# Attention scores as keys by queries in 32-row tiles, with K in natural order and projections of a whole head group

## Chip, cores and metric

The kernel runs on one core of one Trainium2 chip. The metric is the device time of one execution in microseconds (us). A run that is over 1.5% above the fastest of its kernel is called slow, and only fast runs are compared.

Names of the engines: PE is TensorE's matmul side, PEld its weight load, DVE is VectorE, ACT is ScalarE, POOL is GpSimd, SP is SyncE.

## The reference

```python
B, Sq, D = 8, 112, 640
H, Sk, Dh = 32, 512, 192                      # bf16 everywhere
q = (x @ wq).reshape(B, Sq, H, Dh).transpose(0, 2, 1, 3)
scores = einsum("bhqd,bhkd->bhqk", q, k_cache) * Dh ** -0.5
p = softmax(scores)
o = einsum("bhqk,bhkd->bhqd", p, v_cache)
out = o.transpose(0, 2, 1, 3).reshape(B, Sq, H * Dh) @ wo
```

K and V are 50 MB each and every byte of them is used once. The projections are small beside them in bytes, but not in TensorE time: in the kernel before they take 1.55 of the 3.64 us that a pair of heads takes (by the starts of the matmuls, O 3 x (216 + 55) ns and Q 15 x 49).

## The kernel before

The kernel before works on pairs of heads. It computes scores as queries by keys. K comes through a transposing DMA, so that the head dimension lies on the partitions. The four score matmuls of a head contract over 2 x 128 rows although a head has only 192: part of each is padding. The exponentials are then turned round by matmuls against a diagonal matrix that also divides by the sum, and evicted by ScalarE (one head) and VectorE (the other), before PV can use them.

```python
def pe_S(pe, i):                      # scores of two heads, queries x keys
    ...
        pe.matmul(bk[:, 0:256], qs[:, qb, EA[h], :], ktb[:, :, 0, cs], start=True, stop=False)
        pe.matmul(bk[:, 0:256], qs[:, qb, ET[h], :], ktb[:, :, 1, cs], start=False, stop=True)
        pe.matmul(bk[:, 256:512], qs[:, qb, OC[h], :], ktb[:, :, 2, cs], start=True, stop=False)
        pe.matmul(bk[:, 256:512], qs[:, qb, OH[h], :], ktb[:, :, 1, cs], start=False, stop=True).then_inc(sS, 1)

def pe_PT(pe, ip, h):                 # turn the exponentials round
    ...
    for j in range(4):
        mm = pe.matmul(ps[:, 2 + h, j * SQ:(j + 1) * SQ], p_sb[:, pslot, j * 128:(j + 1) * 128],
                       dg[:, dslot, :], start=True, stop=True)

def pe_Q(pe, ip):                     # query projection of two heads, transposed
    ...
    for c in range(3):
        for dc in range(DC):
            lhsT = wq_sb[:, wb, dc, c0 + 128 * c:c0 + 128 * (c + 1)]
            mm = pe.matmul(ps[:, 5, c * SQ:(c + 1) * SQ], lhsT, xT_sb[:, dc, b * SQ:(b + 1) * SQ],
                           start=(dc == 0), stop=(dc == DC - 1))
```

Of the kernel before, what the change touches and what calls it, by code (L numbers as in the profile page):

```python
# [5 lines left out]

BF16 = mybir.dt.bfloat16
F32 = mybir.dt.float32
ACTF = mybir.ActivationFunctionType
ALU = mybir.AluOpType  # L10

DEFAULT_ORDERS = dict(
    PE=[("S", 0), ("PT0", -1), ("PV", -2), ("PT1", -1), ("O", -3), ("Q", 2)],
# [7 lines left out]
def build_mha_kernel(nc, x, k_cache, v_cache, wq, wo, out, cfg=None):  # L21
    cfg = dict(cfg or {})
    B, SQ, D = x.shape
    _, H, SK, DH = k_cache.shape
# [3 lines left out]
    DC = D // 128  # L28
# [8 lines left out]
    scale = float(DH) ** -0.5  # L37
# [31 lines left out]

    with ExitStack() as es:  # L70
        def sb(name, shape, dt):
            return es.enter_context(nc.sbuf_tensor(name, shape, dt))

        def sem(name):
            return es.enter_context(nc.semaphore(name))

        WQC = HG * DH
        wq_sb = sb("wq_sb", [128, 2, DC, WQC], BF16)
        wo_sb = sb("wo_sb", [128, 2, 3 * PPU, D], BF16)
        OUTT = cfg.get("OUTT", False)  # L80
        if OUTT:
            accT = sb("accT", [128, B, DC, SQ], F32)
            oTf = sb("oTf", [128, 2, DC, SQ], BF16)
            acc = None
        else:
            acc = sb("acc", [SQ, B, D], F32)
        xT_sb = sb("xT_sb", [128, DC, B * SQ], BF16)
        kt = [sb(f"kt{j}", [128, 2, 3, G * 128], BF16) for j in range(NKB)]
        vt = [sb(f"vt{j}", [128, G, 768], BF16) for j in range(NVB)]
        qs = sb("qs", [128, NQ, NSLOT, SQ], BF16)  # L90
        s_sb = sb("s_sb", [SQ, NSS, SK], F32)
        p_sb = sb("p_sb", [SQ, NP, SK], BF16)
# [4 lines left out]
        ident = sb("ident", [128, 128], BF16)  # L97
        nmx = sb("nmx", [SQ, NS], F32)
        rsum = sb("rsum", [SQ, NS], F32)
        rinv = sb("rinv", [SQ, NS], F32)  # L100
        ps = es.enter_context(nc.psum_tensor("ps", [128, 8, 512], F32))

        sS = sem("sS"); sPT = sem("sPT"); sPV = sem("sPV"); sO = sem("sO"); sQ = sem("sQ")
        dSM = sem("dSM"); dDG = sem("dDG"); dQC = sem("dQC"); dPTE = sem("dPTE"); dOA = sem("dOA"); dRC = sem("dRC")
        aEX = sem("aEX"); aQE = sem("aQE"); aPTE = sem("aPTE"); aPVE = sem("aPVE")
        gI0 = sem("gI0"); gINIT = sem("gINIT"); dINIT = sem("dINIT")
        sOF = sem("sOF"); aOF = sem("aOF")
        mX = sem("mX")
# [4 lines left out]
        mK = [sem(f"mK{j}") for j in range(NKB)]  # L113
        mV = [sem(f"mV{j}") for j in range(NVB)]
        mOUT = [sem(f"mOUT{j}") for j in range(2)]
# [3 lines left out]
        mWQ = [sem(f"mWQ{j}") for j in range(min(2, NHG) * PPU)]  # L119
        mWO = [sem(f"mWO{j}") for j in range(min(2, NHG) * PPU)]  # L120
# [23 lines left out]
        block = es.enter_context(nc.Block())  # L144

        def W(eng, s, v):
            if v > 0:
                eng.wait_ge(s, v)
# [120 lines left out]
        def act_evacQ(act, ip):  # L269
            W(act, sQ, ip + 1)  # L270
            W(act, sS, 2 * (ip - NQ) + 2)
            act.activation(qs[:, ip % NQ, 0:3, :], ps[:, 5, 0:3 * SQ].rearrange("p (c s) -> p c s", c=3),  # L272
                           ACTF.Copy).then_inc(aQE, 1)

        def act_evacpT0(act, ip):
            W(act, sPT, 2 * ip + 1)
            W(act, sPV, ip - NPT + 1)
            act.activation(pT_sb[:, ip % NPT, 0, :], ps[:, 2, 0:4 * SQ], ACTF.Copy).then_inc(aPTE, 1)  # L278

        def act_exp(act, i, h):  # L280
            Hh = 2 * i + h
            W(act, dSM, Hh + 1)
            W(act, sPT, Hh - NP + 1)
            act.activation(p_sb[:, Hh % NP, :], s_sb[:, Hh % NSS, :], ACTF.Exp,  # L284
                           bias=nmx[:, Hh % NS:Hh % NS + 1], scale=-1.0,
                           accum_out=rsum[:, Hh % NS:Hh % NS + 1]).then_inc(aEX, 1)

        def act_evacPV(act, ip):
            W(act, sPV, ip + 1)
            W(act, sO, ip - NO + 1)  # L290
            act.activation(oT_sb[:, ip % NO, :, :], ps[:, 4, 0:3 * SQ].rearrange("p (c s) -> p c s", c=3),  # L291
                           ACTF.Copy).then_inc(aPVE, 1)

        def act_evacOF(act, ip):
# [3 lines left out]
            W(act, sOF, b + 1)  # L298
            act.activation(o_out[:, b, :], psb[0:SQ, 7, 256:256 + D], ACTF.Copy).then_inc(aOF, 1)

# [3 lines left out]
        def dve_diag(dve, ip, h):  # L304
# [3 lines left out]
            dve.tensor_scalar(dg[:, Hh % ND, :], ident[0:SQ, 0:SQ], rinv[:, Hh % NS:Hh % NS + 1], None,  # L308
                              op0=ALU.mult).then_inc(dDG, 1)

# [17 lines left out]
        def dve_smax(dve, i, h):  # L328
            Hh = 2 * i + h
            W(dve, sS, Hh + 1)  # L330
            W(dve, aEX, Hh - NSS + 1)
            dve.tensor_scalar(s_sb[:, Hh % NSS, :], ps[0:SQ, h, :], -scale, None, op0=ALU.mult,  # L332
                              op1=ALU.min, accum_out=nmx[:, Hh % NS:Hh % NS + 1]).then_inc(dSM, 1)

# [11 lines left out]
        def dve_oacc(dve, ip):  # L346
# [6 lines left out]
            if OUTT:  # L353
# [3 lines left out]
                for k, (src, cs) in enumerate(parts):  # L357
# [6 lines left out]
                    else:  # L364
                        ins = dve.tensor_tensor(dst, src, accT[:, b, cs, :], op=ALU.add)
                ins.then_inc(dOA, 1)
                return
            parts = [(ps[0:SQ, 6, :], slice(0, 512)), (ps[0:SQ, 7, 0:128], slice(512, 640))]
            for k, (src, cs) in enumerate(parts):
# [4 lines left out]
                elif hg < NHG - 1:  # L374
                    ins = dve.tensor_tensor(acc[:, b, cs], src, acc[:, b, cs], op=ALU.add)
                else:
                    ins = dve.tensor_tensor(o_out[:, b, cs], src, acc[:, b, cs], op=ALU.add)  # L377
            ins.then_inc(dOA, 1)
# [5 lines left out]
        psb = ps[:].bitcast(BF16)  # L384
# [27 lines left out]
        def run_program(eng, stages, order, hook=None, post_hook=None):  # L412
            for i in PER:
                if hook is not None:
                    hook(eng, i)
                for st, lag in order:
                    ip = i + lag
                    if ok(ip):
                        stages[st](eng, ip)
                if post_hook is not None:  # L420
                    post_hook(eng, i)
# [24 lines left out]
        def _(act):  # L446
            W(act, dINIT, 1)
            act.activation(dummy[:, 2:3], dummy[:, 0:1], ACTF.Exp)
            run_program(act, ACT_STAGES, orders["ACT"])
# [211 lines left out]
    return nc  # L661


def bass_standalone__mha_block_cached__near_ridge_kernel(
    nc: bass.Bass,
    x: bass.AP,
    k_cache: bass.AP,
    v_cache: bass.AP,
    wq: bass.AP,
    wo: bass.AP,  # L670
    out: bass.AP,
):
    return build_mha_kernel(nc, x, k_cache, v_cache, wq, wo, out)


# [26 lines left out]
```

## Time and profile before

| what | value |
|---|---|
| time, median of 3 runs | 500.46 us (500.19 to 501.19) |
| span of the profiled execution | 499.2 us |
| PE busy, VectorE busy, ScalarE busy | 96%, 89%, 71% |
| PE instructions, matmuls, weight loads and waits (single records) | 14,364 |
| packets of instructions (queue q8) | 56 |

The page of the kernel before, cut to lines that matter here. "busy" is the time and the share of the span, with the number of instructions. The two rows of digits cut the span into 40 slices: the granted TensorE clock, and the mean busy share of the DMA engines, in tenths. The queue row is packets, megabytes and share of 16 engines. The last line is the chain of work that ended last, by engine.

```profile
span 499.2 us, 18678 instructions
PE 479.0 (96%) x6824; PEld 418.9 (84%) x6824; DVE 446.6 (89%) x1610; ACT 355.1 (71%) x898; POOL 71.5 (14%) x133
PEclk9999999999999999999999999999999999999999
DMA  9999999999999999999999999999999999999000
q8 instruction: 56, 0.92, 0.8%
PE 93%; DMA 2%; issue 1%; DVE 1%; POOL 1%; ACT 0%; DVEq 0%; POOLq 0%; ACTq 0%
```

TensorE is busy nearly all the time at full clock (the clock record gives 1.0 for 471 us and 0.5 for the last 2.9), and it is 93% of the chain. So this kernel is bound by TensorE's work. The row "q8 instruction" is easy to pass over: 0.92 MB in 56 packets is 16 KB each, and 14,364 / 56 is 256 instructions of PE for each.

The timeline of PE in the kernel before, one line for each run of like instructions: start, duration, line, operation, output and inputs, shapes, count.

```profile
301.23 0.36 PE L182 MATMUL ps<-dg,p_sb 112*128 112x112 bf16 x4
301.43 0.56 PE L200 MATMUL ps<-pT_sb,vt 128*128 128x112 bf16 x8
301.92 0.39 PE L206 MATMUL ps<-pT_sb,vt 128*64 128x112 bf16 x8
```

The starts tell the price, as the records of matmuls overlap (L200's last 213 ns in the mean and start 49 ns apart at the median): L200 starts 0.49 us before L206 with eight matmuls of 112 columns, 61 ns each with the switch of tile shapes included. There is no pause between groups.

The longest waits of PE in the kernel before: instruction, what ended the wait, total us, times, longest.

```profile
PE ps L402 <- DMA vt<-in_x_dram: 7.2, 1, 7.2
PE ps L262 <- DMA wq_sb<-in_wq_dram: 5.2, 3, 1.9
PE ps L166 <- issue: 1.9, 5, 0.8
```

PE waits about 16 us in all, most of it for first loads. "issue" is time in which the engine waited for nothing that the profile shows; it is 1.9 us here.

### The profile page before, as it was taken

The numbers are of one execution on the slowest core, as the hardware profiler recorded it, in microseconds if no ns is written. First come the engines' busy times: TensorE is split into PE (matmuls) and PEld (weight loads), VectorE is DVE, ScalarE is ACT, GpSimd is POOL, SyncE is SP. The second block draws the span as 40 slices with busy tenths as digits, with TensorE's granted clock in tenths as the row PEclk, the third lists the DMA queues.
The fourth block names the chain that finished last, engine by engine and source line by source line (L and its number), as shares of the span: only waits on it lengthen the run. The fifth ranks groups of instructions, "written<-read, shape, count | busy, mean of one in ns | idle before, by whom it ended". The sixth has DMA issues, their size and how long they took to land.

```text
span 499.2 us, 18678 instructions
## 1 busy us (share of the span) xinstructions
PE 479.0 (96%) x6824; PEld 418.9 (84%) x6824; DVE 446.6 (89%) x1610; ACT 355.1 (71%) x898; POOL 71.5 (14%) x133
## 2 busy tenths in 40 slices
PE   1799999999999999999999999999999999999995
PEld 1788888888888888888888888888888888888884
DVE  2589999998999999999999999999999999999994
ACT  1277777777777777777777777777777777777773
POOL 7110133131000133131000122322000000000000
PEclk9999999999999999999999999999999999999999
DMA  9999999999999999999999999999999999999000
GB/s 227 305 285 239 244 256 274 249 265 292 237 249 263 281 261 259 245 265 251 239 247 236 259 290 279 240 282 260 233 272 254 255 260 255 238 258 261 3 14 25
DMA packets 239738, 119.90 MB, mean 240 GB/s; under 512 B 201840, under 2 KB 236480, under 8 KB 239648
## 3 DMA queue, kind: packets, MB, share of 16 engines
q1 hardware_dynamic: 233472, 101.82, 94.4%
q0 software_dynamic: 6176, 16.88, 11.3%
q8 instruction: 56, 0.92, 0.8%
q14 instruction: 34, 0.28, 0.2%
HBM read 67.21 MB, written 1.15 MB: 137 GB/s over the span
## 4 chain that ended last, share of the span: by engine, by line
PE 93%; DMA 2%; issue 1%; DVE 1%; POOL 1%; ACT 0%; DVEq 0%; POOLq 0%; ACTq 0%
PE ps L262 19%; PE ps L234 16%; PE ps L182 13%; PE ps L200 10%; PE ps L206 8%; PE ps L166 6%; PE ps L169 6%; PE ps L167 6%; PE ps L168 6%; PE ps L235 4%; DMA wq_sb<-in_wq_dram 2%; DVE xT_sb L409 1%; POOL wq_sb L578 0%; DVE s_sb L332 0%; DVE o_out L377 0%
## 5 line engine op out<-in xcount | busy, mean ns | idle before, releaser
L284 ACT ACTIVATE p_sb<-s_sb,nmx 112x512 bf16<-112x512 f32 x256 | 181.6, 712 | 3.1 <-DVE s_sb L332 2.1
L332 DVE TENSOR_SCALAR_CACHE_REDUCE s_sb<-ps 112x512 f32<-112x512 f32 x256 | 166.3, 686 | 16.2 <-PE ps L169 14.0
L278 ACT ACTIVATE pT_sb<-ps 128x448 bf16<-128x448 f32 x128 | 69.5, 543 | 88.4 <-PE ps L182 88.4
L262 PE MATMUL ps<-xT_sb,wq_sb 128*128 128x112 bf16 x1920 | 118.0, 215 | 5.2 <-DMA wq_sb<-in_wq_dram 5.2
L234 PE MATMUL ps<-wo_sb,oT_sb 128*112 128x512 bf16 x384 | 118.3, 380 | 0.0
L262 PEld LDWEIGHTS ps<-xT_sb,wq_sb 128*128 128x128 bf16 x1920 | 103.8, 99 | 16.7 <-DMA wq_sb<-in_wq_dram 4.4
L182 PE MATMUL ps<-dg,p_sb 112*128 112x112 bf16 x1024 | 94.0, 214 | 1.8 <-ACT p_sb L284 1.6
L272 ACT ACTIVATE qs<-ps 128x336 bf16<-128x336 f32 x128 | 57.6, 450 | 45.0 <-PE ps L262 41.8
L338 DVE CAST pT_sb<-ps 128x448 bf16<-128x448 f32 x128 | 79.9, 624 | 5.3 <-PE ps L182 1.4
L235 PE MATMUL ps<-wo_sb,oT_sb 128*112 128x128 bf16 x384 | 83.9, 219 | 0.0
L182 PEld LDWEIGHTS ps<-dg,p_sb 112*128 112x128 bf16 x1024 | 64.5, 98 | 14.4 <-ACT p_sb L284 1.9
L166 PE MATMUL ps<-kt,qs 128*112 128x256 bf16 x256 | 70.8, 277 | 2.5 <-issue 1.9
L200 PE MATMUL ps<-pT_sb,vt 128*128 128x112 bf16 x1024 | 71.8, 213 | 0.1
L167 PE MATMUL ps<-kt,qs 128*112 128x256 bf16 x256 | 70.4, 275 | 0.0
L169 PE MATMUL ps<-kt,qs 128*112 128x256 bf16 x256 | 70.4, 275 | 0.0
L168 PE MATMUL ps<-kt,qs 128*112 128x256 bf16 x256 | 70.3, 275 | 0.0
L234 PEld LDWEIGHTS ps<-wo_sb,oT_sb 128*112 128x112 bf16 x384 | 49.7, 129 | 22.3
L581 POOL DMA_DIRECT2D wq_sb<-in_wq_dram x60 | 32.1, 539 | 188.5 <-DMA kt<-in_k_cache_dram 182.4
L308 DVE TENSOR_SCALAR dg<-ident,rinv 112x112 bf16<-112x112 bf16 x256 | 52.9, 249 | 5.0 <-issue 0.5
L200 PEld LDWEIGHTS ps<-pT_sb,vt 128*128 128x128 bf16 x1024 | 56.5, 98 | 0.9 <-issue 0.5
L291 ACT ACTIVATE oT_sb<-ps 128x336 bf16<-128x336 f32 x128 | 55.3, 432 | 1.7 <-PE ps L206 1.7
L235 PEld LDWEIGHTS ps<-wo_sb,oT_sb 128*112 128x112 bf16 x384 | 50.0, 130 | 0.0
(38 smaller groups left out, 498.5 us busy)
## 6 DMA issues: line engine op xcount, KB each, us to landing
vt<-in_v_cache_dram SPq DMA_DIRECT2D x64, 768.0 KB, 5.8
wq_sb<-in_wq_dram POOLq DMA_DIRECT2D x60, 96.0 KB, 5.3
wo_sb<-in_wo_dram POOLq DMA_DIRECT2D x24, 160.0 KB, 5.6
wo_sb<-in_wo_dram POOLq DMA_DIRECT2D x32, 80.0 KB, 5.1
wq_sb<-in_wq_dram POOLq DMA_DIRECT2D x4, 480.0 KB, 10.2
wo_sb<-in_wo_dram POOLq DMA_DIRECT2D x4, 320.0 KB, 10.9
out_dram<-o_out SPq DMA_DIRECT2D x8, 140.0 KB, 4.4
kt<-in_k_cache_dram SPq DMA_TRANSPOSE x64, 9.9
```

What stands on the lines that cost most here:

```text
L166: pe.matmul(bk[:, 0:256], qs[:, qb, EA[h], :], ktb[:, :, 0, cs], start=True, stop=False)
L167: pe.matmul(bk[:, 0:256], qs[:, qb, ET[h], :], ktb[:, :, 1, cs], start=False, stop=True)
L168: pe.matmul(bk[:, 256:512], qs[:, qb, OC[h], :], ktb[:, :, 2, cs], start=True, stop=False)
L169: pe.matmul(bk[:, 256:512], qs[:, qb, OH[h], :], ktb[:, :, 1, cs], start=False, stop=True).then_inc(sS, 1)
L182: mm = pe.matmul(ps[:, 2 + h, j * SQ:(j + 1) * SQ], p_sb[:, pslot, j * 128:(j + 1) * 128], dg[:, dslot, :], start=True, stop=True)
L200: pe.matmul(ps[:, 4, oc * SQ:(oc + 1) * SQ], vtb[:, u, q * 192: q * 192 + 128], pT_sb[:, ptb, h, j * SQ:(j + 1) * SQ], start=(j == 0), sto ...
L234: pe.matmul(ps[0:SQ, 6, :], oT_sb[:, ob, c, :], wo_sb[:, wb, 3 * lp + c, 0:512], start=first, stop=last)
L235: mm = pe.matmul(ps[0:SQ, 7, 0:128], oT_sb[:, ob, c, :], wo_sb[:, wb, 3 * lp + c, 512:640], start=first, stop=last)
L262: mm = pe.matmul(ps[:, 5, c * SQ:(c + 1) * SQ], lhsT, xT_sb[:, dc, b * SQ:(b + 1) * SQ], start=(dc == 0), stop=(dc == DC - 1))
L284: act.activation(p_sb[:, Hh % NP, :], s_sb[:, Hh % NSS, :], ACTF.Exp, bias=nmx[:, Hh % NS:Hh % NS + 1], scale=-1.0, accum_out=rsum[:, Hh % ...
L332: dve.tensor_scalar(s_sb[:, Hh % NSS, :], ps[0:SQ, h, :], -scale, None, op0=ALU.mult, op1=ALU.min, accum_out=nmx[:, Hh % NS:Hh % NS + 1]). ...
L338: dve.tensor_copy(pT_sb[:, ip % NPT, 1, :], ps[:, 3, 0:4 * SQ]).then_inc(dPTE, 1)
```

## The change

The intent is to take padding and turning-round out of TensorE. The work unit becomes four heads of one batch (64 units). K is loaded as it lies in memory and transposed by VectorE (256 instructions of 128 x 384), so that each head owns 32 partitions. Scores come out as keys by queries, in tiles of 32 rows: four tiles, one for each head, are meant to work beside each other in the array. The exponentials are then already in the layout that PV wants, so the turning-round matmuls, their evictions, the max pass and the diagonals go. PV, the sums (a matmul with ones) and both projections are tiles of 32 columns. The projections take all 896 query rows by whole head groups. A check of the sums' range, and the old kernel behind a branch that isn't taken, are there for safety.

```diff
+ # Q: x @ wq, four 32-column tiles, weights taken every sixth column
+     for dc in range(DC):
+         for a in range(4):
+             mm = pe.matmul(ps[32 * a:32 * a + 32, bk, 0:HQ],
+                            wqs[:, g % 2, dc, DH * a + c:DH * (a + 1):6],
+                            xT[:, dc, HQ * h:HQ * (h + 1)], start=(dc == 0), stop=(dc == DC - 1))
+ # O: output projection, four 32-column tiles
+     for c in range(6):
+         for a in range(4):
+             mm = pe.matmul(ps[32 * a:32 * a + 32, bk, 0:HO],
+                            oT[:, c, 128 * m + 32 * a:128 * m + 32 * a + 32],
+                            wos[:, g % 2, c, HO * h:HO * (h + 1)], start=(c == 0), stop=(c == 5))
+ # S: scores, four 32-row tiles
+     for t in range(4):
+         for c in range(6):
+             for a in range(4):
+                 p = slice(32 * a, 32 * a + 32)
+                 mm = pe.matmul(ps[:, a, SQ * t:SQ * (t + 1)], kt[u % 2][p, t, c // 2, :, c % 2],
+                                qT[g % 2][p, c, SQ * b:SQ * (b + 1)], start=(c == 0), stop=(c == 5))
+ ...
+ # sums and PV, four 32-column tiles
+     for t in range(4):
+         for a in range(4):
+             mm = pe.matmul(ps[32 * a:32 * a + 32, 5, 3 * SQ:4 * SQ], ones[:], pT[u % 2][:, a, t, :],
+                            start=(t == 0), stop=(t == 3))
+ ...
+     for c in range(6):
+         if c == 3:
+             W(pe, vRC, u + 1)
+         for t in range(4):
+             for a in range(4):
+                 mm = pe.matmul(ps[32 * a:32 * a + 32, 4 + c // 3, SQ * (c % 3):SQ * (c % 3 + 1)],
+                                vs[u % NV][:, a, DH * t + c:DH * (t + 1):6], pT[u % 2][:, a, t, :],
+                                start=(t == 0), stop=(t == 3))
+ # order of a unit on PE
+     for u in range(NU):
+         do_S(u)
+         its = items_at[u]                 # parts of Q and O that fill the wait for exp
+         for it in its[:-1]: do(it)
+         do_sum(u)
+         for it in its[-1:]: do(it)
+         do_PV(u)
+ # VectorE: transpose of K
+     src = kr[u % NK][:].bitcast(I32).rearrange("p (s t) (i c) -> p t c s i", t=4, c=3)[:, t]
+     dst = kt[u % 2][:].bitcast(I32).rearrange("p t c (j s) e -> p t c s (j e)", s=4)[:, t]
+     dve.transpose(dst, src).then_inc(vKT, 1)
+ ...
- build_mha_kernel(nc, x, k_cache, v_cache, wq, wo, out)
+ build_main(nc, x, k_cache, v_cache, wq, wo, out, flag)
+ with nc.If(raised != 0):                  # not taken here
+     build_mha_kernel(nc, x, k_cache, v_cache, wq, wo, out)
```

In every one of the five loops a matmul of 128 became four of 32. A matmul is two instructions on PE, the weight load and the matmul itself (17,956 of each in the trace of the changed kernel).

## The prediction

> **What bounds the kernel now.** TensorE. The page's busy part shows PE 96%; the chain of waits is PE 93%. In the timeline one pair of heads takes 3.64 us, steadily: scores 8 matmuls at 109 ns, transposing matmuls 8 at 49, PV 8 at 49 plus 8 narrow ones, O 3 x (216+55), Q 15 x 49. 128 pairs are about 466 us; start and tail are 33. VectorE is busy 89%, ScalarE 71%. DMA shows 9 tenths throughout at 240 GB/s, but 304 us (per engine, summed from packet records) are 196,608 packets of 256 B of the DMA transpose, 18 ns each.
>
> **What the change does.** Removed: the half-empty score matmuls (256 rows of contraction for 192), the transposing matmuls and both pT evictions, max pass, diagonals, q copies, DMA transpose. Added: a VectorE transpose of K (256 of 128x384 int32), reciprocals of 128x112, and a skipped fallback. Moved: every matmul becomes four tiles (32 rows or 32 columns).
>
> **Do four tiles run as one?** The narrow PV matmuls (128x64) are already column-tiled: single records show the second of a pair 3 to 4 ns after the first and 49 ns per pair, the price of one full matmul of 112. [...]this trace shows two. A switch of tiling costs about 0.11 us (200->206 takes 143 ns instead of 49, 206->182 145).
>
> **Cost of one unit (4 heads, one batch; 64 units), TensorE, estimated from those gaps.** S 24 groups x 49 = 1.18 us, sums 4 x 49 = 0.20, PV 1.18, Q 1.5 items x 5 x 189 = 1.42, O 1.75 x 6 x 136 = 1.43, two switches 0.22: 5.6 us against 7.28 now.
>
> **What is not hidden.** The sums wait for four exps of 128x448: the PSUM copies of that shape on ScalarE start 0.44 us apart and take 0.54, and start 0.25 us after the last matmul's start: 2.2 us after S, in which only 1.6 to 1.9 us of O or Q stand. About 0.4 us of stall in most units: 6.0 us. VectorE per unit, estimated: NM 672 elements 0.79, [...]O evictions 0.74[...]: 4 to 4.5 us. It fits, but the reciprocal gates the second half of PV with little slack. DMA: 1.82 MB per unit; 1536 B packets take 65 ns on 16 engines, 378 GB/s, 4608 B ones 346: 5.0 to 5.3 us, under TensorE by a little.
>
> 64 x 6.05 = 387 us, first scores at about 16 us (14.2 now), tail with output, flag and branch 12: **415 us**, ratio 1.2. Range 388 to 470. Faster by over 2%: 0.91; within 2%: 0.04; slower: 0.05.
>
> **What would show it.** Right: groups of four matmuls 49 ns apart; exp about 0.54; [...]PE idle before the sums released by ScalarE, 20 to 30 us in all; a unit of about 6 us; DMA at 290 GB/s. Wrong: gaps within a group well over 4 ns (instruction issue or weight loads: 8 instructions per 49 ns); transposes of 0.8 us or more (12 and 16 byte strides), which put VectorE into the chain; PE waiting for kr or vs.
>
> **What would make it wrong.** If four loads and four matmuls can't issue in 49 ns, S, sums and PV (2.6 us a unit) grow in proportion: at 98 ns the total is near 580 us. If transposes take 0.9 us, a unit is over 7.5 us and the gain is gone. If DMA reaches only 300 GB/s, a unit is 6.1 us, no worse.

VectorE's sum came to 4 to 4.5 us a unit; of its terms 0.79 + 0.74 = 1.53 us stand, so that "It fits" is not shown. The two that stand are estimates: in the trace of before VectorE's instructions of 512 and of 128 elements start 0.60 and 0.20 us before the next (medians where they follow directly, L375), and a straight line through these gives 0.77 us for 672 elements and 0.70 for 1.75 times 320. No term of TensorE's sum, 5.6 us and with its waits 6.05, is cut; the 415 us is 64 x 6.05 + 16 + 12. That four tiles cost what two do was my estimate from the pairs.

## The result

The changed kernel gives a correct result and takes **664.02 us** (median of 4 runs, 661.45 to 671.69; the slowest of them is not compared). The ratio to the kernel before is 1.3246, with a 95% interval of 1.32 to 1.3293. All ratios here are the mean time of one kernel's fast runs over that of the other's of the same rounds, so not quite the ratio of the medians quoted, which take in every run, slow ones too. The kernel is a third slower, where it was predicted to be 17% faster.

The page of the changed kernel, with the rows that answer to those of before, and the costliest group (line, engine, operation, names, shapes, count, busy us, mean ns of one, idle before it).

```profile
span 659.1 us, 37838 instructions
PE 452.6 (69%) x17956; PEld 348.8 (53%) x17956; DVE 349.3 (53%) x505; ACT 174.0 (26%) x357; POOL 106.4 (16%) x199
PEclk9988999998879889788889888899899898897898
DMA  9965546645466545665457455475446464455400
q8 instruction: 142, 2.33, 1.4%
L921 DVE STREAM_TRANSPOSE kt<-kr 128x384 int32<-128x384 int32 x256 | 212.5, 882 | 0.0
```

No engine is near its limit. PE is busy 69%, VectorE 53%, ScalarE 26%, and DMA, which was at nine tenths, is at four to six. Everything became lighter and the kernel became longer. The clock row has dropped from 9 to 8 and 7 in places. The instruction packets went from 56 to 142.

The waits of PE in the changed kernel (same columns as before):

```profile
PE ps L830 <- issue: 86.1, 41, 4.4
PE ps L810 <- issue: 31.6, 19, 3.4
PE ps L851 <- issue: 21.9, 15, 2.7
PE ps L840 <- issue: 15.4, 7, 3.4
PE ps L851 <- DVE rinv L936: 14.5, 19, 1.6
PE ps L796 <- issue: 11.8, 8, 2.3
PE ps L840 <- ACT pT L893: 7.3, 17, 1.9
```

L830 is S, L810 O, L851 PV, L840 the sums, L796 Q. The waits that the prediction looked for are there, for the reciprocal (14.5 us) and for exp (7.3 us), and they are small. The five lines with "issue" add up to 166.8 us: PE stands still, and nothing that the profile shows as a dependency holds it.

The timeline of PE in the changed kernel; the brackets give the idle time before a run of instructions.

```profile
314.01 0.40 PE L796 MATMUL ps<-xT,wqs 128*32 128x448 bf16 x4
315.60 0.97 PE L796 MATMUL ps<-xT,wqs 128*32 128x448 bf16 x16 [1.18 <-issue]
316.35 1.40 PE L851 MATMUL ps<-pT,vs 128*32 128x112 bf16 x96
317.68 0.38 PE L830 MATMUL ps<-qT,kt 32*128 32x112 bf16 x16
320.54 1.85 PE L830 MATMUL ps<-qT,kt 32*128 32x112 bf16 x80 [2.48 <-issue]
322.31 2.73 PE L810 MATMUL ps<-wos,oT 128*32 128x320 bf16 x48
```

The pauses lie in the middle of a part: after 4 of the 20 matmuls of one Q item, and after 16 of the 96 of S. No semaphore is waited for there. And after the second pause the same work is slow: 80 matmuls of S in 1.8 us, where 96 of PV took 1.33 just before.

Three stretches around that second pause: busy us and count of each engine, then the granted clock, the DMA share and GB/s.

```profile
core 0: us, PE busy (x) PEld busy (x) DVE busy (x) ACT busy (x) POOL busy (x), PEclk, DMA share, GB/s
316.75:318.34 1.59, 1.30 (x99) 1.08 (x87) 0.55 (x1) 0.41 (x1) 0.60 (x1) 1.00 0.97 397
318.00:320.80 2.80, 0.32 (x28) 0.27 (x26) 2.09 (x3) 0.00 (x0) 0.00 (x0) 1.00 0.76 219
320.90:324.20 3.30, 3.30 (x100) 2.37 (x92) 0.04 (x1) 1.80 (x4) 0.00 (x0) 0.50 0.22 79
```

During the pause the DMA engines are 76% busy. After it TensorE is granted half its clock. The clock records give 0.5 for pieces of 3.413 us (27 of them) or two together (5, and one of 6.376), 133 us in all. They don't say what brings a drop about. Before each of the 33 drops to half clock PE was idle for 1.96 to 3.35 us of the 3.413 us before it; the pause here was 2.48 us. At half clock groups of S and PV start 93 ns apart, of O 267 and of Q 373, where they start 49, 136 and 189 ns apart at full clock (the commonest spacings).

### What stands at the pauses

The trace also has single records: every PE instruction with its start, and every instruction packet with its start and landing. Counting PE's instructions from the first, 80% of the pauses longer than 0.8 us (85 of 106) stand at an instruction whose number leaves 193 (give or take 3) when divided by 256. A packet of 16 KB for 256 instructions is 64 bytes each. So the pauses stand at the borders of packets. They also end in step with the packets: nine tenths of these 85 end between 1.26 and 1.59 us after a packet landed (the median is 1.42). (That the number is 193 and not 0 is an offset that stays the same through the whole program.) Here are five borders, taken from single records (us from the start of the span). A block is the 256 instructions of one packet.

```
block   last start before it   packet starts   packet landed   its first start
61           297.59                294.88          295.80          297.59
62           299.28                300.58          301.52          302.81
65           314.04                313.16          314.15          315.60
66           317.85                318.34          319.30          320.53
67           324.74                321.77          322.81          324.74
```

At blocks 62, 65 and 66 PE runs out, and resumes 1.2 to 1.5 us after the packet landed. At 61 and 67 the packet landed 1.8 and 1.9 us ahead and nothing is lost. The packet for block 67 started 1.2 us after block 66 had begun (321.77 - 320.53), but the one for block 66 started 2.7 us after block 65 had begun (318.34 - 315.60). While that packet was overdue, the DMA engines were 97% busy (the first of the three stretches above). Over the whole trace the packet for a block starts at the earliest about 1.15 us after PE enters the block before, wherever PE then had to wait for it. (In 20 of 141 blocks it started sooner, one of them 0.27 us before PE entered the block before; PE waited for none of those.) So I read the trace as one block being asked for ahead. The packet takes about 1.0 us, and then about 1.4 us pass before its first instruction runs. So where PE starves, blocks follow each other about 3.5 us apart or more slowly: the 5th percentile of the packets' spacing is 3.45 us, the shortest 3.14. (Single blocks began as little as 2.3 us after the one before, where the block before had itself begun late.) In S, PV and the sums 256 instructions are 32 groups of four tiles at 49 ns, 1.6 us of work. In the kernel before a packet lasted 7.95 us (median).

The following table is computed the same way for every kernel run, and is used below. "Delay" is from the start of a block's first instruction to the start of the packet for the next block. "Gaps" are pauses over 0.5 us on PE that end 1.1 to 1.9 us after an instruction packet landed. "Half-clock" is the time in which TensorE was granted half its clock. The single records have in some kernels one packet more than the page counts. The column of times mixes medians of several runs with single runs (marked s); "before" is as it ran beside the others. Delays counted again from the traces came out up to 0.2 us different, by which instruction is taken to open a block; no reading rests on that much.

```
kernel                time us    PE instr packets  spacing, us  delay, us         gaps      half-clock
                                                   median/p5    p25/median/p75    n, us     us
before                500.8      14364    56       7.95/6.05    2.09/3.47/4.39     1,   1     3
changed               664.0      36171   143       4.14/3.45    1.17/1.36/2.58    93, 193   133
qo_full               607.2      29259   116       4.76/3.43    1.22/1.75/2.90    63, 133   113
kt_third              649.6      36171   143       3.97/3.45    1.15/1.31/2.26    99, 195   121
all_full              428.0 s     9291    38      11.47/7.93    0.37/1.54/2.41     2,   3     9
all_full_kt_third     407.3 s     9291    38      10.34/7.72    0.74/1.42/2.24     4,   4     6
spread_tiled          683.3      36171   143       3.96/3.41    1.15/1.36/3.02   101, 222   150
spread_full           605.0      29259   116       4.84/3.52    1.21/1.75/3.62    74, 143    92
before_q_tiled        661.4      25884   101       6.59/3.69    1.67/3.40/4.49    52, 112    56
kt_strides            655.7 s    36171   143       4.00/3.47    1.17/1.35/2.55    94, 191   129
spread_tiled_nodata   572.2 s    36171   143       3.83/3.39    1.14/1.23/1.50   124, 158    32
after_split           637.0      36171   143       4.32/3.46    1.23/1.65/2.15    97, 187    94
spread_tiled_split    627.7      36171   143       4.13/3.40    1.21/1.54/2.01   124, 199    51
spread_full_split     540.2      29259   116       4.38/3.46    1.22/1.73/2.31    74,  98    26
v2                    549.8      23115    92       5.29/3.95    1.36/2.18/3.46    38,  83    77
v2_ktold              472.9      23115    92       4.75/3.59    1.03/1.47/2.52    23,  35    22
```

In the changed kernel 193 us are gaps at packet borders, and 133 us run at half clock, where groups take about twice as long (93 ns for 49). An estimate from those: 659 - 193 - 133/2 = about 400 us (16 us of the half-clock time lie in pauses, so it takes off a little too much). That is close to the predicted 415.

### The profile page after: what moved, and what is told of

It is laid out like the page before. It is cut to its first block, busy times and chain, and to the rows that moved or that the text cites. A ratio compares the mean times of both kernels' runs of the same rounds, so it can differ in the third digit from the quotient of the medians.

```text
span 659.1 us, 37838 instructions
## 1 busy us (share of the span) xinstructions
PE 452.6 (69%) x17956; PEld 348.8 (53%) x17956; DVE 349.3 (53%) x505; ACT 174.0 (26%) x357; POOL 106.4 (16%) x199
## 3 DMA queue, kind: packets, MB, share of 16 engines
HBM read 117.54 MB, written 1.15 MB: 180 GB/s over the span
## 5 line engine op out<-in xcount | busy, mean ns | idle before, releaser
L921 DVE STREAM_TRANSPOSE kt<-kr 128x384 int32<-128x384 int32 x256 | 212.5, 882 | 0.0
L893 ACT ACTIVATE pT<-ps 128x448 bf16<-128x448 f32 x256 | 119.5, 548 | 291.8 <-PE ps L830 291.8
L830 PE MATMUL ps<-qT,kt 32*128 32x112 bf16 x6144 | 104.7, 220 | 89.6 <-issue 86.1
L810 PE MATMUL ps<-wos,oT 128*32 128x320 bf16 x2688 | 129.2, 341 | 32.5 <-issue 31.6
L830 PEld LDWEIGHTS ps<-qT,kt 32*128 32x128 bf16 x6144 | 87.4, 99 | 97.6 <-issue 92.6
L796 PE MATMUL ps<-xT,wqs 128*32 128x448 bf16 x1920 | 127.5, 397 | 11.8 <-issue 11.8
L851 PE MATMUL ps<-pT,vs 128*32 128x112 bf16 x6144 | 107.0, 224 | 36.6 <-issue 21.9
L851 PEld LDWEIGHTS ps<-pT,vs 128*32 128x32 bf16 x6144 | 101.8, 126 | 48.8 <-issue 25.7
L810 PEld LDWEIGHTS ps<-wos,oT 128*32 128x32 bf16 x2688 | 75.3, 107 | 72.3 <-issue 43.0
L796 PEld LDWEIGHTS ps<-xT,wqs 128*32 128x32 bf16 x1920 | 66.1, 128 | 42.4 <-issue 28.0
L840 PE MATMUL ps<-pT,ones 128*32 128x112 bf16 x1024 | 29.5, 228 | 22.7 <-issue 15.4
L840 PEld LDWEIGHTS ps<-pT,ones 128*32 128x32 bf16 x1024 | 22.6, 105 | 35.2 <-issue 16.8
```

The source lines that it names most:

```text
L796: mm = pe.matmul(ps[32 * a:32 * a + 32, bk, 0:HQ], wqs[:, g % 2, dc, DH * a + c:DH * (a + 1):6], xT[:, dc, HQ * h:HQ * (h + 1)], start=(dc ...
L810: mm = pe.matmul(ps[32 * a:32 * a + 32, bk, 0:HO], oT[:, c, 128 * m + 32 * a:128 * m + 32 * a + 32], wos[:, g % 2, c, HO * h:HO * (h + 1)] ...
L830: mm = pe.matmul(ps[:, a, SQ * t:SQ * (t + 1)], kt[u % 2][p, t, c // 2, :, c % 2], qT[g % 2][p, c, SQ * b:SQ * (b + 1)], start=(c == 0), s ...
L840: mm = pe.matmul(ps[32 * a:32 * a + 32, 5, 3 * SQ:4 * SQ], ones[:], pT[u % 2][:, a, t, :], start=(t == 0), stop=(t == 3))
L851: mm = pe.matmul(ps[32 * a:32 * a + 32, 4 + c // 3, SQ * (c % 3):SQ * (c % 3 + 1)], vs[u % NV][:, a, DH * t + c:DH * (t + 1):6], pT[u % 2] ...
L893: act.activation(pT[u % 2][:, a, :, :].rearrange("p t q -> p (t q)"), ps[:, a, 0:4 * SQ], ACTF.Exp, scale=scale).then_inc(aEX, 1)
```

## The experiments

In the quoted expectations letters stand for theories. Two stood at the start. **F**: PE starves for instructions, because tiling by four multiplied them by 2.5 (14,364 to 36,171), and the half clock follows from the pauses. **D**: VectorE's transposes of K, at 882 ns each over the 0.8 us that the prediction called wrong, hold PE, and "issue" hides it. The expectations name two more rivals: **W**, that the tiles themselves are slow in the array, and **C**, that each packet costs a fixed time of about 4.5 us. A later form of F, called **Q**, came after the second group of runs: the packets themselves start late when data loads are moving. The gaps and packets of each run are in the table above.

### First group: is it the instructions, or the transposes?

**qo_full** writes Q and O as full matmuls of 128 columns. The array gets the same columns and the result is the same, with 6,912 instructions fewer.

```diff
-  for a in range(4):
-      mm = pe.matmul(ps[32*a:32*a+32, bk, 0:HQ], wqs[:, g % 2, dc, DH*a + c:DH*(a+1):6], ...)
+  mm = pe.matmul(ps[:, bk, 0:HQ], wqs[:, g % 2, dc, c:4 * DH:6], ...)
   ...
-  for a in range(4):
-      mm = pe.matmul(ps[32*a:32*a+32, bk, 0:HO], oT[:, c, 128*m + 32*a:128*m + 32*a + 32], ...)
+  mm = pe.matmul(ps[:, bk, 0:HO], oT[:, c, 128 * m:128 * m + 128], ...)
```

> Q and O as single 128-column matmuls instead of four 32-column tiles: the same products, a correct result, about 29,260 instructions on TensorE instead of 36,171, that is 114 fetch packets of 256 instructions instead of 143. Theory F (TensorE starves for its instructions: packets land no closer than about 3.5 us apart): gaps that end about 1.4 us after an instruction packet lands stay, but fewer; at the present 4.5 us a packet 530 to 560 us, at best 114 x 3.5 + 25 = 425. Rival W (the tiles themselves are slow, the array is the limit): no gain, three more changes of tiling a unit at 0.11 us make it 20 us slower, about 680. Rival D (VectorE's 882 ns transposes are the limit): unchanged, 650 to 665.

It took 607.2 us (runs from 599.45 us; ratio to the kernel before 1.2071, 1.1982 to 1.216). Undoing the tiling of Q and O alone gives 57 us back, so F has the direction right. The size was missed: I expected 530 to 560. Q and O were the parts in which a block lasts long (a group takes 189 and 136 ns there, against 49), so taking their instructions away leaves the short blocks of S, PV and the sums as short as before. The gaps fell only from 193 to 133 us.

**kt_third** lets VectorE transpose only a third of K from the third unit on. The scores are then wrong in principle, and the result was still reported correct: the tolerance of the comparison doesn't see this, which matters below. (It also means that "correct" says little about the scores of the changed kernel itself.)

```diff
+  if u >= 2:
+      src, dst = src[:, 0:1], dst[:, 0:1]
   dve.transpose(dst, src).then_inc(vKT, 1)
```

> From unit 2 on each transpose of K covers 128 of 384 columns (wrong result on purpose); TensorE's instructions are untouched. Theory F: 640 to 665 us, unchanged within 3%, although VectorE loses over 100 us of work. Rival D: the transposes were the limit, 530 to 580 us. Rival W: unchanged.

It took 649.6 us (ratio 1.29, 1.2778 to 1.3022). VectorE's busy time fell by 107 us (349.3 to 242.4 in the page) and the kernel gained 14 us. D is out as the cause.

**all_full** makes S, the sums and PV full 128 x 128 matmuls too, one for each group of four. Its output is wrong, which doesn't matter for the time. The array's time for a group is meant to stay the same; only the instructions fall to a quarter.

```diff
-  for t in range(4):
-      for c in range(6):
-          for a in range(4):
-              mm = pe.matmul(ps[:, a, SQ*t:SQ*(t+1)], kt[u % 2][p, t, c // 2, :, c % 2], qT[g % 2][p, c, ...], ...)
+  for n in range(24):
+      r, c = n % 16, n // 4
+      a, t = divmod(r, 4)
+      mm = pe.matmul(ps[:, a, SQ*t:SQ*(t+1)], kt[u % 2][:, t, c // 2, :, c % 2], qT[g % 2][:, c, ...], start=True, stop=True)
   # sums and PV in the same way: one matmul of 128 columns where four of 32 were
```

> Each group of four tiled matmuls becomes one full 128x128 matmul over the same number of streamed columns (wrong result on purpose): the array's time per group is the same 49, 136 and 189 ns, the instructions fall to about 9,300, 37 packets. Theory F: no gaps behind instruction packets, 400 to 440 us, about what the prediction's sum said. Rival W, if tiles run as slow as four matmuls: also a large gain, but then the groups of the changed kernel would have to be longer than 49 ns. Rival D: over 600 us.

It took 428.03 us (one run), against the 415 us predicted for the change. Its page and its waits of PE:

```profile
span 426.4 us, 10958 instructions
PE 371.6 (87%) x4516; PEld 292.3 (69%) x4516; DVE 332.2 (78%) x505; ACT 173.2 (41%) x357; POOL 106.4 (25%) x199
PEclk9999999999999999999999999999999999999998
q8 instruction: 37, 0.61, 0.6%
```

```profile
PE ps L834 <- ACT pT L886: 23.2, 47, 1.9
PE ps L844 <- DVE rinv L929: 16.0, 38, 1.4
```

The clock stays at 9, the longest wait with "issue" is 0.7 us in all, and what remains are the two waits that the prediction named. Everything else of the change is in this kernel: the same loads, transposes, exponentials, projections and order (only the first exp of a unit now waits for the whole of S). So the time above 428 us comes with the number of PE instructions. This run takes the tiles away together with the instructions, so by itself it doesn't tell F from W. W is out because groups of four tiles start 49 ns apart in the changed kernel's own trace, the price of one full matmul, and because the pauses stand at the borders of packets.

**all_full_kt_third** puts both edits together.

> The last two together (wrong result on purpose). If with instructions out of the way VectorE's transposes are the next limit (4 x 0.83 + 0.82 + 0.78 + 0.74 = 5.7 us a unit, estimated from the records), this is 20 to 60 us faster than the full-array kernel; if TensorE's own work and the waits for exps are, within 2% of it.

It took 407.25 us (one run, wrong), 20.8 us less than all_full. Once the instructions arrive in time, the transposes are worth 5%. They were not what made the changed kernel slow.

### Second group: is it a fixed floor for each block?

The first form of F had a fixed floor of 3.5 us for each block, and blocks of very uneven work. It followed that a more even order of the work would help by itself.

**spread_tiled** keeps all instructions and changes their order on PE: half of S, an item of Q or O, the other half of S, an item, the sums and half of PV of the unit before, an item, the other half of PV. O moves one unit later, and the evictions follow. **spread_full** adds the full matmuls of qo_full.

```diff
-  do_S(u)
-  for it in its[:-1]: do(it)
-  do_sum(u)
-  for it in its[-1:]: do(it)
-  do_PV(u)
+  do_S(u, 0);            do(its[0])
+  do_S(u, 1);            do(its[1])
+  do_sum(u - 1);  do_PV(u - 1, 0);  do(its[2])
+  do_PV(u - 1, 1);       # and what items are left
```

> The changed kernel with the same instructions, tiles and number of them (about 36,200 on TensorE), only in another order: the scores of a unit in two halves, the value products of the unit before in two halves, a projection item between each of them, so that the cheap instructions (49 ns for 8) never stand 384 in a row. A correct result. Theory F (a block of 256 instructions can't begin sooner than about 3.5 us after the one before): 141 blocks x 3.5 = 495 us plus start and tail, 510 to 550, since each block now holds close to the same work. Rival C (each instruction packet costs a fixed time, 4.5 us, whatever stands in it): unchanged, 650 to 665. Rival W (the tiles or their switches are slow): 24 more changes of tiling in 8 units, slower than 660. Part of the gain could come from the waits for exps, which go away: at most the 20 to 40 us that the waits view of the changed kernel puts down to exp and reciprocal.

> The same order with Q and O as full 128-column matmuls, correct, about 29,300 instructions. Theory F: 114 blocks x 3.5 = 400 us as a floor; the array's own work is then 6.2 us a unit with its changes of tiling, VectorE's 5.7: 430 to 475 us, faster than the kernel before (500). Rival C: 607, as with full Q and O in the old order. Rival W: over 600.

spread_tiled took 683.3 us (ratio 1.3627, 1.356 to 1.3693) and spread_full 605.0 (1.2057, 1.1999 to 1.2115). The even order made the changed kernel slower and did nothing for the version with full projections. A fixed floor as the whole limit is refuted (510 to 550 and 430 to 475 us had been expected). The table shows what had grown from the changed kernel to spread_tiled: the 75th percentile of the packets' delay, from 2.58 to 3.02 us, and the gaps, from 193 to 222 us.

**before_q_tiled** goes the other way round. It takes the kernel before and tiles only its Q by four. Nothing else of the change is in it, and the result is the same.

```diff
-  lhsT = wq_sb[:, wb, dc, c0 + 128*c:c0 + 128*(c+1)]
-  mm = pe.matmul(ps[:, 5, c*SQ:(c+1)*SQ], lhsT, ...)
+  for a in range(4):
+      c1 = c0 + 128*c + 32*a
+      mm = pe.matmul(ps[32*a:32*a+32, 5, c*SQ:(c+1)*SQ], wq_sb[:, wb, dc, c1:c1+32], ...)
```

> The kernel before with its Q projection cut into four 32-column tiles, correct: 196 instead of 106 matmul and load instructions... per pair of heads in loads and matmuls 106 to 196, about 25,900 in all, 101 packets instead of 56, but a block of 256 still holds about 4.7 us of work. Theory F: few or no gaps behind instruction packets; only two more changes of tiling a pair, 128 x 0.22 = 28 us: 515 to 540. Rival C (a packet costs its 4.5 us): 45 more packets, about 200 us more. Rival W: tiled Q groups of four well over 49 ns.

It took 661.4 us (ratio 1.3224, 1.313 to 1.3318), as slow as the changed kernel. I had expected 515 to 540, so this is the largest miss, and it is a miss of size: the direction is F's. W fails here too: the tiled Q groups start 49 ns apart. Its first wait of PE:

```profile
PE ps L263 <- issue: 62.5, 34, 3.5
```

L263 is the tiled Q. In the table the delay of its packets has a median of 3.40 us, against 1.36 in the changed kernel. The kernel before had that same delay (3.47) and lost nothing by it, because it had 7.95 us of work for each packet.

Rival C's numbers came nearer than F's in this group: it had said unchanged (650 to 665), 607 and about 700 us, and 683.3, 605.0 and 661.4 were measured. But a fixed cost of a packet isn't what the traces show. The median spacing is 3.96 us in spread_tiled and 6.59 in before_q_tiled, and below the same 143 packets take 111 us less when the data loads are gone.

**kt_strides** asks a side question. The four transposes of a unit get four pairs of strides: as in the change, write contiguous, read contiguous, both contiguous. All move 128 x 384 elements of 4 bytes.

> The changed kernel with the four transposes of a unit in four forms of the same 128x384 (wrong order of data on purpose): t=0 as it is (read stride 12 bytes, write stride 16), t=1 written contiguously, t=2 read contiguously, t=3 both. [...]if 32-bit transposes are that slow by themselves [...], all four take about 880. The total stays within 3% of 660 under theory F either way.

Its groups on VectorE by form: L924 as in the change (read every 12 bytes, written every 16), L926 written contiguously, L928 read contiguously, L930 both.

```profile
L928 DVE STREAM_TRANSPOSE kt<-kr 128x384 int32<-128x384 int32 x64 | 58.0, 906 | 0.0
L924 DVE STREAM_TRANSPOSE kt<-kr 128x384 int32<-128x384 int32 x64 | 55.6, 868 | 0.0
L926 DVE STREAM_TRANSPOSE kt<-kr 128x384 int32<-128x384 int32 x64 | 39.7, 620 | 0.0
L930 DVE STREAM_TRANSPOSE kt<-kr 128x384 int32<-128x384 int32 x64 | 35.4, 554 | 0.0
```

The write stride of 16 bytes costs about 250 ns of the 868 (868 - 620), and 352 beside a contiguous read (906 - 554). The read stride of 12 bytes costs 66 ns where the write is contiguous (620 - 554) and nothing where it isn't (868 against 906). Contiguous it is 554 ns, and 248 of the 314 ns above that go with the write stride alone. So the long transpose is mostly a matter of the write stride. The kernel's time was 655.69 us (one run), beside 664: again nothing that explains the slowdown.

### Third group: do the packets queue behind data?

What made delays longer in some kernels? Blocks in the single records were sorted by the bytes of K and V data that moved around the block's start (0.5 us before to 0.8 us after). In spread_tiled the median delay is 1.16 us for under 50 KB (73 blocks), 3.95 us for 150 to 250 KB (10) and 2.62 us for 350 to 600 KB (39). In the changed kernel it is 1.19 us for under 50 KB, and 1.3 to 2.7 us in the classes above, without a steady rise. So theory Q was formed: an instruction packet starts later when K and V loads are under way, because it waits for them. The waiting itself is not in the records; that was my guess. Two edits test this.

**spread_tiled_nodata** loads K and V only into the first buffers and never again (the result is wrong). All instructions remain.

```diff
   if u >= NK:
       W(sp, vKT, 4 * (u - NK + 1))
+      return            # K's and V's later loads are left out
```

> The evenly ordered kernel with all its tiles, but K and V are loaded for the first units only and used again (wrong data on purpose). The last call refuted a fixed 3.5 us for an instruction block: even order gained nothing (683 us), and the kernel before with a tiled Q, 4.7 us of work a block, stalled too. In the traces an instruction packet starts 1.15 us after TensorE enters the block before it where little other data moves, but 2 to 4.3 us after where K and V are on the way. Theory Q (the instruction packet queues behind the data loads): without loads every packet starts about 1.15 us after, blocks follow at 3.5 us: 141 x 3.5 = 495 plus start and tail, 505 to 545. If the fetch itself is late for another reason (the sequencer), the starts stay spread and the time stays over 640.

It took 572.15 us (one run), 111 us less than spread_tiled, though a little above my 505 to 545. Its page and its waits of PE:

```profile
DMA  8931000300004000220002200022000100000100
q8 instruction: 142, 2.33, 1.7%
```

```profile
PE ps L854 <- issue: 49.8, 46, 2.3
PE ps L832 <- issue: 43.9, 43, 1.8
```

With the DMA engines nearly empty the delay's 75th percentile is 1.50 us (3.02 with data), the gaps fall from 222 to 158 us, and the half-clock time from 150 to 32. This shows two things. The data traffic does lengthen the delay. And almost without data traffic 158 us of gaps are left: one block ahead, with about 3.4 us from packet to packet (5th percentile 3.39), is too little for this many instructions by itself.

**after_split**, **spread_tiled_split** and **spread_full_split** keep all data, and cut the K and V loads into four DMAs of 192 KB each (and wq into five, wo into three), so that, if theory Q holds, less can stand ahead of an instruction packet. In the packet records only K's and wo's packets become shorter by it (6144 bytes to 1536, 7680 to 2560); V's and wq's were 1536 bytes before and stay so.

```diff
-  sp.dma_start(kr[u % NK][:]..., k_cache[b, 4*g:4*g+4]...).then_inc(mK[u % NK], 16)
+  for q in range(4):
+      sp.dma_start(kr[u % NK][:, 4*q:4*q+4, :]..., k_cache[b, 4*g:4*g+4]...[:, 4*DH*q:4*DH*(q+1)]).then_inc(mK[u % NK], 16)
```

> The changed kernel with each load of K and V in four DMAs of 192 KB, wq in five, wo in three; everything else as it was, a correct result. [...]the delay of packet starts at the 75th percentile falls from 2.6 to under 1.8 us, total 580 to 630. If the instruction packet waits for all that was issued before it, whatever its pieces, nothing changes: 650 to 665.

> Even order, all tiles, loads split as above, correct. Theory Q with waits of one small packet: 141 blocks x 3.5 to 4 us: 520 to 580, against 683 unsplit. If all of the backlog is waited for: 670 to 690.

> Even order, Q and O full, loads split, correct. Theory Q with waits of one small packet: 114 blocks x 3.5 to 4 us, or TensorE's own 6.2 us a unit: 430 to 490, faster than the kernel before. If all of the backlog is waited for: 595 to 610.

| kernel | without split | with split | ratio to before, with split |
|---|---|---|---|
| changed | 664.0 | 637.0 | 1.2697 (1.2633 to 1.276) |
| spread_tiled | 683.3 | 627.7 | 1.2543 (1.2472 to 1.2615) |
| spread_full | 605.0 | 540.2 | 1.082 (1.0759 to 1.0882) |

All three gained, by 27, 56 and 65 us, and all three stayed above what I expected (580 to 630, 520 to 580, 430 to 490). The 95th percentile of the delay fell from 3.70 to 2.99 us in the changed kernel's order and from 4.25 to 2.58 in the even order; its 75th percentile in after_split is 2.15 us, where under 1.8 was expected. So the direction of Q holds, and the even order now helps a little (637.0 to 627.7, under the 2% at which kernels are told apart here). But the split takes away only the long delays, and with them mainly the half-clock time (150 to 51 us in the even order). The many gaps at the least spacing remain.

The runs after_split and qo_full had their profiled execution slow, so their rows in the large table come from a slow run; their times don't.

### Fourth group: a version built on this

If instructions are what is short, fewer of them should win. **v2_ktold** combines the full matmuls for Q and O, the even order (with the two halves of PV together again) and the split loads, and does PV and the sums in two tiles of 64 columns instead of four of 32, so that PV is 24 groups of two tiles in a unit where it was 24 groups of four, with half the instructions. PE has 23,115 instructions then instead of 36,171. The reciprocal grows from 112 to 224 columns (816 ns in the changed kernel, 1551 in v2_ktold). Rows of wo are loaded in the matching order.

```diff
   # PV: two tiles of 64 columns
-  for a in range(4):
-      pe.matmul(ps[32*a:32*a+32, 4 + c // 3, ...], vs[u % NV][:, a, DH*t + c:DH*(t+1):6], pT[u % 2][:, a, t, :], ...)
+  for e in range(2):
+      a = 2 * k + e
+      pe.matmul(ps[64*e:64*e+64, 4 + r // 4, ...], vs[u % NV][:, a, DH*t + c:DH*(t+1):3], pT[u % 2][:, a, t, :], ...)
```

**v2** adds one thing: each head's K is dealt onto its 32 partitions by one of the four DMAs so that the transposes write contiguously.

> A version made for the cause found: even order, Q and O full, split loads, and the value products and sums in 64-column tiles (two at a time, same array time, half the instructions), so 22,900 instructions or 90 packets; K's keys are dealt to the partitions so that the transposes write contiguously (620 instead of 868 ns in the test of strides). Correct result. Theory Q: 90 blocks at 3.5 to 4.5 us no longer bound a unit (1.4 blocks, 4.9 to 6.3 us); TensorE's own work with six changes of tiling is 6.3 us: 440 to 480 us, ratio to the kernel before 0.88 to 0.96. If the number of instructions is not what holds it, it stays near 540.

> The same with the transposes as the changed kernel has them (16-byte write stride, 868 ns). If VectorE (6.4 us a unit with them, 5.4 without, estimated from the records) is by now the limit, this is 20 to 60 us slower than the last; if instruction fetch or TensorE still is, within 2%.

v2_ktold took **472.9 us** (median of 5 runs, 469.55 to 482.75; the slowest is the profiled one). The ratio to the kernel before is 0.9457 (0.9416 to 0.9498), and the result is correct. It beats both kernels, by 5% and by 29% (472.9 / 664.0 = 0.71). Against spread_full_split, from which it differs mainly in the tiles of PV and the sums, 29,259 PE instructions became 23,115 and 540.2 us became 472.9. v2 took 549.8 us (ratio 1.0998, 1.0939 to 1.1056), against 440 to 480 expected, and neither of the outcomes named for v2_ktold came (20 to 60 us slower than v2, or within 2% of it).

The page of v2_ktold and its longest wait of PE:

```profile
span 480.4 us, 25206 instructions
PE 426.9 (89%) x11428; PEld 310.3 (65%) x11428; DVE 388.1 (81%) x505; ACT 173.4 (36%) x357; POOL 173.2 (36%) x199
PEclk9999999998999999999999979999899999999998
q8 instruction: 91, 1.49, 1.3%
```

```profile
PE ps L828 <- issue: 14.2, 13, 2.5
```

PE is busy 89% again, at nine tenths of full clock or more in all slices but four, with 91 packets; the longest wait with "issue" is 14.2 us, and 35 us are gaps. This profile is of the slow run, so it shows the kernel rather at its worst.

v2 has the faster transposes, 682 ns against 873, and is 77 us slower. Between the two profiles the share of the data queue differs, 89.9% against 76.0%, the time from issue to landing of a K load, 6.3 us against 4.1 (median), and the packets' delay, 2.18 us against 1.47 (median); gaps are 83 us against 35. Both have 70,656 data packets of 1536 bytes, but they take 100 ns each in v2 and 65 in v2_ktold (medians). That fits theory Q, by which K's new way of loading keeps the DMA engines busier and the instruction packets pay. But the two kernels differ in the loads and in the transposes' write stride together, so this is argued from the traces and not shown by an experiment.

One caution on v2: as kt_third passed with scores that were wrong in principle, the comparison doesn't confirm that v2 deals K rightly. v2_ktold keeps the changed kernel's K path.

## Why the prediction was wrong

What was right, point by point:

- **What bounds the kernel before.** TensorE, 93% of the chain.
- **Four tiles run as one.** Groups of four start 49 ns apart in S and PV (medians of over 1,100 groups each), 189 in Q and 136 in O, as predicted. The trace of before showed this for two tiles; this trace shows it for four.
- **Exp and NM.** Exp was predicted at 0.54 us and took 548 ns. NM was given 0.79 and took 858 ns. (The reciprocal took 816 ns.)
- **The sum of it all.** With the instructions taken away, the same work took 428 us (all_full), 3% above the predicted 415, with 23.2 us of waits for exp (20 to 30 predicted) and 280 GB/s of DMA (290 predicted).

What was wrong:

- **The step that failed** is the cost of one unit on TensorE, 5.6 us and with its waits 6.05, added up from groups at 49, 189 and 136 ns as if their instructions were always there. A unit took 9.81 us (median from the first score of one to that of the next), though the groups cost what was said. The section on what would make it wrong came near it with "If four loads and four matmuls can't issue in 49 ns". That was treated as a rate at which PE can issue what it has, with 5% for the chance that the kernel gets slower. PE does issue eight instructions in 49 ns, so the sign that the text looks for (gaps within a group) doesn't appear. What can't keep up is the supply: one block of 256 instructions ahead, about 3.5 us from block to block where PE starves, against 1.6 us of work in a block of tiles. The sum had no term for it. It measured 193 us in gaps and 133 us at half clock, of which about half is loss (an estimate: groups start 93 ns apart there, not 49).
- **The transposes** took 882 ns, over the 0.8 us that the text called wrong. The consequence it drew ("the gain is gone", an estimate) didn't follow: kt_third gained 14 us and all_full_kt_third 20.8. They were longer than the text allowed, and off the chain.
- **DMA** was to run at 290 GB/s and ran at 184. That is a result of the slowdown; in all_full it is 280.

The trace of before would have shown it. It had 56 instruction packets, one for each 7.95 us at the median, and each started 3.47 us (median) after PE had entered the block before, and was still in time (it landed at least 1.50 us before its block's first start). The change multiplies PE's instructions by 2.5 and shortens their work, so an estimate from those numbers, before any run, is 56 x 2.5 = 140 packets, and at the predicted 415 us 3.0 us for each: less than the delay of 3.47 us alone. (In the changed kernel the delay then was 1.36 us at the median, so this estimate gives the sign and not the size.)

What stays open: why only one block is asked for ahead; why the even order without the split had longer delays (75th percentile 2.58 to 3.02 us), though it moves the same data; how much of v2's loss is the K load and how much the stride; and why qo_full, before_q_tiled, the splits and v2 all stayed above what I had expected. The direction of each followed the theory, but no sum of mine foretells the size of the gaps. That data loads lengthen the delay of instruction packets is shown by the run without data (75th percentile 1.50 us against 3.02) and supported by the splits (4.25 to 2.58 us at the 95th in the even order); that the packets wait for the data inside the DMA engines was not observed.

## What to carry to other kernels

Count instructions as well as array time when you tile matmuls: here four tiles of 32 cost the array what one full matmul costs (49 ns a group in S and PV), and cost the instruction supply four times as much (eight instructions for two). Divide the work in us by the number of 256-instruction blocks, in each stage and not on average: here a stage with under about 3.5 us for each block starved, and data loads raised that to 5 us and more in spread_tiled (an estimate: a delay of 2.6 to 4 us there, and 1.0 for the packet and 1.4 after it as in the changed kernel). Use tiles only where they save padding (S here), use full or 64-column ones elsewhere (spread_full_split to v2_ktold: 540.2 to 472.9 us), and where PE shows long "issue" waits in the middle of a part (86.1 us in S here), compare the row of instruction packets before looking for a slow engine.
